# Attention with a gated MLP on one core: new last denominators, x chunk 1 loaded in two parts, other planner numbers for four blocks

## The chip, the cores and the metric

The kernel runs on one core of one Trainium2 chip. The metric is the device time of one execution in microseconds, the median of several. Before the change it is 414.47 us, the median of three runs from 414.26 to 415.19.

## The reference, cut to what matters

```python
x = A_x                                   # 1 x 2048 x 448, bf16
xn = _layernorm(x, axis=-1)
qkv = xn @ wqkv                           # 16 heads of 28
scores = einsum("bhqd,bhkd->bhqk", q, k) * 28 ** -0.5
s = einsum("bhqk,bhkd->bhqd", softmax(scores), v) @ wo
h = gelu(xn @ w1 + b1)                    # 448 -> 1792, tanh form
g = silu(h @ w2 + b2)                     # 1792 -> 448
return x + s * g
```

The softmax's denominator is divided out after the product with v: the kernel sums exp(scores) for each query and head and multiplies the head's output by the reciprocal.

## The kernel before

The 2048 rows are cut into four chunks of 512, the 16 heads (28 wide, padded to 32) into four groups of four. A **block** is one group and one chunk of queries, 16 in all, numbered group by group. A block has 64 **score tiles** (one head of the group by 128 keys by 512 queries), so there are 1024, counted by m. Four heads lie in the four row groups of the PE array, so their score matmuls run side by side (L1700). ACT takes the exponential of two or three tiles in one instruction (L1754); groups of four tiles, the "late" ones, are instead approximated on DVE (L2034 for the scores, L2107 for copies that are added up on PE). Then PE multiplies the exponentials by v (L2282), with a column of twos beside v that yields the denominators. Of all this the layer norm, the projections, the MLP with its gelu (between about 224 and 251 us) and the output projection are spread beside the exponentials.

The order is made when the program is built, by a planner in Python. Each piece of work is a generator that yields tasks with an engine, the buffers that it reads and writes, an estimated duration and a priority; `run` puts down the task that can start first, with rules for priorities, and the instructions go into each engine's queue in that order. The numbers of these rules (`BPN`) are set anew for each block from a row of `BP`; `NQ[b]` is the number of times that the planner tries to make a late group in block b, evenly spaced over its tiles (`p_late`, `pick`). The estimates set the order alone: on the chip every instruction waits on semaphores.

**The start.** `loads` issues x chunk 0 in three parts, the first heads' weights on ACT's and SP's queues (L952), then x chunk 1 whole on SP (L940). `p_ln` takes the statistics of each tile of 128 rows on DVE (`bn_stats`, L1016), `p_ln2` takes the logarithm and the exponential on ACT for the inverse root (L1052, L1054) and normalizes on DVE (L1071); PE transposes (L1204), and ACT or DVE moves the result to xnT (L1216, L1217). The projections follow, and the first scores and exponentials.

ACT's function table is set by name at two places: line 933, before everything (`natural_log_exp_and_others`), and line 1594, after the gelu (`exp_and_others`).

**The tail.** The last block is cut in three parts by queries: 0 to 255, 256 to 383 and 384 to 511. For the third part `p_den` makes the denominators ahead of the product with v: DVE copies what has been accumulated so far (L2194), PE spreads the copy's denominator rows over each head's 32 rows in a bank called `K.den`, and `t_ones` adds the last tiles by matmuls with a matrix of twos (L2227). `p_epi4` copies the sums out of PSUM (L2311 by ACT for this part, L2314 by DVE for the others); `p_norm4` takes the reciprocal on DVE (L2332) and multiplies (L2337). `p_last` projects with wo (through `_mm`, L129), and `t_oev` writes the tile out: either DVE multiplies by the gate from PSUM (L2403), or, for the tiles in `PATH` and after the last exponential has been put down, ACT copies (L2399) and DVE multiplies (L2401); then DVE adds x (L2409) and SP stores (L2413). The gate of the last tile is made beside that: Tanh on ACT (L1661), a product on POOL (L1666), an add on DVE (L1671).

## Time and profile before

| | |
|---|---|
| median of the runs | 414.47 us |
| the profiled execution | 414.64 us |
| its span, first to last instruction | 412.8 us |
| granted TensorE clock | 0.999 |
| first exponential of a score starts | 13.27 us |
| exponentials of scores (L1754) | 354 instructions, 776 tiles of 512 columns |
| approximated on DVE (L2034) | 248 tiles |
| loads of ACT's function table | 3, of 1.28 us each |

Times are microseconds from the first instruction of the profiled execution. PE is the matmul engine, PEld its weight loads, ACT, DVE, POOL and SP the others; a q behind an engine's name is its DMA queue. A group's row shows line, engine, operation, what it writes and reads, shapes, and how many; behind it busy time, the mean in ns and the idle time before, with what ended it. A timeline's row begins with start and length. In the stretches, the columns are the stretch, its length, the busy time of PE, PEld, DVE, ACT and POOL with the number of instructions, the granted clock, the share of the DMA engines and GB/s. An engine's share of the span is an average; what a change is worth is read from the stretch in which it lies.

### The profile page before, as it was taken

The numbers are of one execution on the slowest core, as the hardware profiler recorded it, in microseconds if no ns is written. First come the engines' busy times: TensorE is split into PE (matmuls) and PEld (weight loads), VectorE is DVE, ScalarE is ACT, GpSimd is POOL, SyncE is SP. The second block draws the span as 40 slices with busy tenths as digits, with TensorE's granted clock in tenths as the row PEclk, the third lists the DMA queues.
The fourth block names the chain that finished last, engine by engine and source line by source line (L and its number), as shares of the span: only waits on it lengthen the run. The fifth ranks groups of instructions, "written<-read, shape, count | busy, mean of one in ns | idle before, by whom it ended". The sixth has DMA issues, their size and how long they took to land.

```text
span 412.8 us, 14654 instructions
## 1 busy us (share of the span) xinstructions
PE 394.0 (95%) x6146; PEld 143.4 (35%) x6146; DVE 345.1 (84%) x599; ACT 401.5 (97%) x411; POOL 193.8 (47%) x218
## 2 busy tenths in 40 slices
PE   5999999999999999999999999999999999999995
PEld 3543232333322233232224553332333223333453
DVE  7958798896679888989898117999998999899986
ACT  5899999999999999999999999999999999999995
POOL 6594656649972563255632411156156014553041
PEclk9999999999999999999999999999999999999999
DMA  7801110001000010100330000220010003200073
GB/s 240 301 4 39 6 31 2 23 12 26 21 3 30 2 28 7 33 2 2 100 105 16 28 3 6 54 54 17 16 31 2 29 6 58 72 16 14 18 144 98
DMA packets 18640, 17.56 MB, mean 43 GB/s; under 512 B 8925, under 2 KB 15277, under 8 KB 18542
## 3 DMA queue, kind: packets, MB, share of 16 engines
q1 hardware_dynamic: 16878, 13.78, 11.4%
q0 software_dynamic: 1008, 2.49, 3.5%
q8 instruction: 49, 0.80, 0.8%
q10 hardware_dynamic: 688, 0.34, 0.3%
q14 instruction: 17, 0.14, 0.1%
HBM read 12.54 MB, written 2.88 MB: 37 GB/s over the span
## 4 chain that ended last, share of the span: by engine, by line
PE 71%; ACT 15%; DVE 6%; issue 5%; DMA 1%; POOL 1%; SPq 0%; DVEq 0%; ACTq 0%; POOLq 0%
PE ring L129 33%; PE ring L1700 19%; PE ring L2282 16%; ACT P L1754 8%; ACT h L1754 5%; DMA x_sb<-in_A_x_dram 1%; PE ring L1513 1%; DVE st L1016 1%; ACT xnT L1754 1%; DVE x_sb L2034 1%; PE ring L1122 1%; DVE h L2034 0%; PE ring L1089 0%; POOL h L1075 0%; DVE vaug L1475 0%
## 5 line engine op out<-in xcount | busy, mean ns | idle before, releaser
L1754 ACT ACTIVATE P<-ring 128x1024 bf16<-128x1024 f32 (+1 forms) x235 | 248.9, 1166 | 1.5 <-PE ring L2282 0.3
L1700 PE MATMUL ring<-qT,kT 32*128 32x512 bf16 (+2 forms) x1132 | 131.4, 359 | 5.6 <-ACT P L1754 1.9
L1754 ACT ACTIVATE h<-ring 128x1024 bf16<-128x1024 f32 (+1 forms) x79 | 85.7, 1177 | 0.4 <-PE ring L2282 0.3
L1700 PEld LDWEIGHTS ring<-qT,kT 32*128 32x128 bf16 x1132 | 36.4, 91 | 120.5 <-ACT P L1754 60.4
L2034 DVE TENSOR_SCALAR vaug<-ring 128x512 uint16<-128x512 f32 x88 | 58.6, 685 | 6.6 <-PE ring L1700 4.6
L129 PE MATMUL ring<-xnT,w 128*32 128x512 bf16 x864 | 57.6, 381 | 0.4 <-ACT h L1754 0.2
L129 PE MATMUL ring<-w,h 128*32 128x448 bf16 x896 | 55.5, 355 | 0.2 <-DVE x_sb L2034 0.2
L2282 PE MATMUL ring<-P,vaug 128*32 128x512 bf16 (+2 forms) x599 | 53.7, 352 | 0.1
L2377 POOL TENSOR_TENSOR qT<-x_sb,E_sb 128x512 bf16<-128x512 f32 x15 | 17.8, 1183 | 65.2 <-PE ring L2282 29.0
L2366 POOL TENSOR_TENSOR rc<-rs,mone 128x16 f32<-128x16 bf16 x11 | 32.4, 2947 | 29.2 <-DMA rs<-E_sb 27.6
L1754 ACT ACTIVATE xnT<-ring 128x1024 bf16<-128x1024 f32 (+1 forms) x40 | 44.0, 1128 | 0.0
L2034 DVE TENSOR_SCALAR w<-ring 128x512 uint16<-128x512 f32 x52 | 34.7, 686 | 2.7 <-PE ring L1700 2.1
L129 PEld LDWEIGHTS ring<-xnT,w 128*32 128x32 bf16 x864 | 20.5, 96 | 26.1 <-issue 6.1
L129 PEld LDWEIGHTS ring<-w,h 128*32 128x32 bf16 x896 | 18.0, 95 | 22.8 <-issue 14.0
L2034 DVE TENSOR_SCALAR h<-ring 128x512 uint16<-128x512 f32 x32 | 21.3, 685 | 3.8 <-PE ring L1700 3.6
L2282 PE MATMUL ring<-h,vaug 128*32 128x512 bf16 (+1 forms) x209 | 23.9, 379 | 0.5 <-ACT P L1754 0.4
L1415 DVE CAST qT<-ring 128x512 bf16<-128x512 f32 x15 | 10.3, 689 | 15.3 <-PE ring L129 14.9
L2282 PEld LDWEIGHTS ring<-P,vaug 128*32 128x32 bf16 x599 | 15.9, 95 | 14.3 <-issue 6.9
L1421 POOL TENSOR_TENSOR qsq<-qT 128x512 bf16<-128x512 bf16 x12 | 12.5, 1039 | 17.9 <-DVE qT L1415 17.9
L1527 DVE CAST h<-ring 128x512 bf16<-128x512 f32 x24 | 16.4, 688 | 5.0 <-PE ring L129 4.9
L2034 DVE TENSOR_SCALAR x_sb<-ring 128x512 uint16<-128x512 f32 x28 | 18.6, 683 | 2.5 <-PE ring L1700 1.6
L129 PE MATMUL ring<-xnT,wk 128*32 128x512 bf16 x232 | 17.9, 383 | 0.0
(245 smaller groups left out, 639.6 us busy)
## 6 DMA issues: line engine op xcount, KB each, us to landing
x_sb<-recs SPq DMA_DIRECT2D x60, 64.0 KB, 2.0
w<-in_B_w_dram SPq DMA_DIRECT2D x1, 1568.0 KB, 8.7
x_sb<-in_A_x_dram SPq DMA_DIRECT2D x3, 448.0 KB, 6.8
w<-in_B_w_dram SPq DMA_DIRECT2D x1, 1344.0 KB, 8.1
out_dram<-in_A_x_dram SPq DMA_DIRECT2D x2, 448.0 KB, 10.2
out_dram<-h POOLq DMA_DIRECT2D x4, 224.0 KB, 6.6
out_dram<-h SPq DMA_DIRECT2D x8, 112.0 KB, 1.8
xnT<-wq POOLq DMA_DIRECT2D x1, 512.0 KB, 6.3
```

The lines of the kernel that those rows point to most:

```text
L129: ins = eng.matmul(out[q:q + 32, :], w[:, q:q + 32], x, tile_position=(0, q), start=start, stop=stop, skip_group_check=True)
L1016: yield _Task(DVE, lambda eng, i=i, t=t: eng.bn_stats(K.st6[:, i, :], K.x_sb[:, c, t, :]), [K.b_x[c] if c else K.b_x0[h] if t else K.b_x0t ...
L1122: return eng.matmul(bank, w[sl, 3, g * 128:(g + 1) * 128], K.xnT[sl, 3, c * 512:(c + 1) * 512], tile_position=pos, start=False, stop=True, ...
L1415: yield _Task(DVE, lambda eng: eng.tensor_copy(qb, bank), [tok], [qr], 0.7, 0.0, dp)
L1421: yield _Task(POOL, lambda eng: eng.tensor_tensor(qs, qb, qb, ALU.mult), [qr], [tq], 1.1, 0.05, 2, port=True)
L1527: yield _Task(DVE, lambda eng: eng.tensor_copy(dst, bank), [tok], wr, 0.69, 0.0, 2)
L1700: return eng.matmul(dst, K.kT[32 * j:32 * j + 32, g, t * 128:(t + 1) * 128], K.qT[32 * j:32 * j + 32, g, c * 512 + q0:c * 512 + q0 + nq], ...
L1754: return eng.activation(reg[:, i0:i0 + n, :], src, ACTF.Exp, scale=SM_SCALE)
L2034: yield _Task(DVE, lambda eng: eng.tensor_scalar(K.part(u, k).bitcast(dt.uint16), K.like(u, bank), SM_SCALE * LOG2E * 128.0, (127.0 - EXP_ ...
L2282: return eng.matmul(acc[32 * j:32 * j + 32, q0:q0 + nq], w, ap[:, col:col + nq] if len(ap.shape) == 2 else ap[:, col // 128:(col + nq) // ...
L2366: yield _Task(POOL, lambda eng: eng.tensor_tensor(K.rc[:, :], K.rs[:, :], K.mone[:, 0:1].to_broadcast([128, 16]), ALU.pow), [K.b_srs, K.b_ ...
L2377: yield _Task(POOL, lambda eng: eng.tensor_tensor(dst, K.rb, E, ALU.mult), [K.b_rb, tE], [K.b_onT[g][c]], 1.15, 0.05, 1, port=True)
```

## The change

It has four parts.

- **The start.** x chunk 1 is loaded in two DMAs: its tile 0 on ACT's queue, behind the weights, with a buffer and a semaphore of its own (`b_x1t`, `s_x1t`); tiles 1 to 3 on SP. The statistics and the normalization of that tile wait for the new semaphore.
- **Planner numbers.** Rows 12 to 15 of `BP` get other values (three unused rows at the end go), and `NQ[13]` is 8 instead of 9.
- **The last denominators.** They are made in two PSUM banks, 64 columns each (`RS`), and each of the last matmuls with twos becomes two. DVE takes the reciprocal of the first half; ACT takes the logarithm of the second half and the exponential of its negative. DVE multiplies by the sums straight from PSUM, so ACT's copy of them goes.
- **Output tiles.** (1,3) and (3,2) leave `PATH`, (3,1) joins it; the add of x for (2,0) goes to POOL. A third way of adding x, on PE, is there for tiles in `PADD`, which is empty.

```diff
-    (2, 1, 0, 2.679, 7, 0.134, 1, 0.031, 0.063, 0.302, -0.231, 18, 3, 0.532, 3, 7, 0.134, 4, 7, 4, 7, 0.691, 0.51, 81, 20, 0, 1, 3.888, 2, 0, 7.133, 12, 3.0),
-    (3, 1, 1, 0.982, 7, 0.12, 1.551, 0.011, 0.163, 1.176, 0.806, 12, 3, 0.03, 4, 4, 0.112, 1, 7, 5, 14, 0.77, 0.506, 46, 23, 1, 1, 4.944, 4, 0, 4.0, 33, 2.058),
-    (3, 1, 0, 3.94, 9, 0.129, 1.365, 0.096, 0.166, 0.546, -0.231, 13, 2, 0.532, 1, 7, 0.15, 4, 8, 12, 4, 0.672, 0.667, 75, 16, 1, 1, 4.005, 1, 1, 7.133, 13, 3.12),
-    (2, 1, 1, 2.679, 30, 0.129, 1, 0.096, 0.247, 0.047, 0.61, 13, 5, 0.532, 3, 7, 0.061, 4, 7, 4, 13, 0.821, 0.7, 75, 14, 1, 1, 3.78, 3, 0, 7.133, 24, 3.0),
+    (2, 1, 0, 2.679, 7, 0.134, 1, 0.021, 0.063, 0.302, -0.231, 18, 3, 0.532, 3, 7, 0.134, 4, 7, 4, 7, 0.691, 0.408, 81, 20, 0, 1, 3.888, 2, 0, 7.133, 12, 3.0),
+    (3, 1, 1, 0.982, 7, 0.12, 1, 0.011, 0.163, 1.176, 0.806, 12, 3, 0.03, 4, 4, 0.112, 1, 7, 5, 14, 0.77, 0.506, 46, 23, 1, 1, 4.944, 4, 0, 4.0, 33, 2.058),
+    (3, 1, 0, 3.94, 9, 0.11, 1.365, 0.096, 0.166, 0.546, -0.5, 13, 2, 0.532, 1, 7, 0.099, 4, 8, 12, 4, 0.672, 1.086, 75, 16, 1, 1, 4.005, 1, 1, 7.133, 16, 3.12),
+    (2, 1, 1, 2.679, 30, 0.129, 1, 0.11, 0.247, 0.047, 0.61, 13, 5, 0.532, 3, 12, 0.061, 4, 7, 4, 13, 0.821, 0.7, 75, 14, 1, 1, 4.2, 3, 0, 7.133, 24, 3.0),
-NQ = (14, 4, 4, 4, 7, 14, 7, 16, 8, 15, 5, 9, 6, 9, 12, 8)
+NQ = (14, 4, 4, 4, 7, 14, 7, 16, 8, 15, 5, 9, 6, 8, 12, 8)
+RS = 64
+PADD = ()
-PATH = {(1, 2): 'D', (1, 3): 'D', (2, 0): 'D', (2, 1): 'D', (2, 2): 'D', (2, 3): 'D', (3, 2): 'D', (3, 3): 'D'}
-XADD = ()
+PATH = {(1, 2): 'D', (2, 0): 'D', (2, 1): 'D', (2, 2): 'D', (2, 3): 'D', (3, 1): 'D', (3, 3): 'D'}
+XADD = ((2, 0),)
...
-        ld(K.x_sb[:, 1, :, :], xr[1], K.s_x[1], [K.b_x[1]], 6.5)
+        K.dma(ACT, lambda eng: eng.dma_start(K.x_sb[:, 1, 0, :], xr[1][:, 0, :]), K.s_x1t, writes=[K.b_x1t], land=6.5)
+        ld(K.x_sb[:, 1, 1:4, :], xr[1][:, 1:4, :], K.s_x[1], [K.b_x[1]], 6.5)
...
-        K.den = yield ("bank", lambda: K.ready([K.b_E[0]]), 1)
-        den, td = K.den
-        yield _Task(PE, lambda eng: _mm(eng, den[:, 0:128], K.selb[:, :], Ea, True, False), [K.b_E[0], K.b_selb], [td], 0.1, 0.12, 1)
+        K.den = []
+        for c0, c1 in ((0, RS), (RS, 128)):
+            x = yield ("bank", lambda: K.ready([K.b_E[0]]), 1)
+            K.den.append(x)
+            yield _Task(PE, lambda eng, d=x[0], c0=c0, c1=c1: _mm(eng, d[:, c0:c1], K.selb[:, :], Ea[:, c0:c1], True, False), [K.b_E[0], K.b_selb], [x[1]], 0.08, 0.12, 1)
...
-        if s == 2 and EA:
-            yield _Task(ACT, lambda eng: eng.activation(K.E_sb[:, 1, sl], bank[0][:, sl], ACTF.Copy), [bank[1]],
-                        [K.b_E4[t] for t in ts] + [K.b_E[1]], 0.3, 0.0, 0)
...
+        if s == 2:
+            K.E_done = NBLK - 1 + s
+            yield from K.p_norm3(*bank)
+            K.banks.append(bank)
+            return
...
+    def p_norm3(self, acc, ta):
+        K = self
+        g, c = G - 1, C - 1
+        (d0, td), (d1, te) = K.den
+        R = K.rf[:, 1, :]
+        K.b_rf3.r += K.b_rf[1].r + [K.b_rf[1].w]
+        K.b_rf3.tr = K.b_rf[1].tr
+        yield _Task(ACT, lambda eng: eng.activation(R[:, RS:128], d1[:, RS:128], ACTF.Ln), [te], [K.b_rf3], 0.2 + 0.00085 * (128 - RS), 0.0, 0)
+        yield _Task(DVE, lambda eng: eng.reciprocal(R[:, 0:RS], d0[:, 0:RS]), [td], [K.b_rf[1]], 0.06 + 0.00705 * RS, 0.0, HOT)
+        yield _Task(ACT, lambda eng: eng.activation(R[:, RS:128], R[:, RS:128], ACTF.Exp, scale=-1.0), [], [K.b_rf3], 0.2 + 0.00085 * (128 - RS), 0.0, 0)
+        K.hot = {DVE: max(K.tE[DVE], K.b_rf3.tw + SEM, ta.tw + SEM)}
+        K.banks += K.den
+        dst = K.qT[:, g, c * 512 + 384:c * 512 + 512]
+        yield _Task(DVE, lambda eng: eng.tensor_tensor(dst, acc[:, 384:512], R, ALU.mult), [ta, K.b_rf[1], K.b_rf3, K.b_qT[g][c]],
+                    [K.b_on4[3]], 0.3, 0.0, HOT)
+        K.hot = {PE: K.b_on4[3].tw + SEM}
+        K.hot[DVE] = K.hot[PE] + 0.43
+        K.on4[3] = True
```

More of the change, by code (lines that the diff above doesn't have):

```diff
@@ L422, in run @@
             self.settle()
-            if self.next_m >= MTOT and all(p[3].prio >= 90 if isinstance(p[3], _Task) else p[3][0] == "bank" and self.lq_end and not self.lq for p in self.procs):
+            if self.next_m >= MTOT and not self.px and all(p[3].prio >= 90 if isinstance(p[3], _Task) else p[3][0] == "bank" and self.lq_end and not self.lq for p in self.procs):
                 return
@@ L2218, in t_ones @@
         K = self
-        den, td = K.den
+        cut = (0, RS, 128)
         fl, rd = [], []
@@ L2324, in p_norm4 @@
         E, tE = K.E_sb[:, 1, 128 * t:128 * (t + 1)], K.b_E4[t]
[L2325 to L2330 removed]
+        bank, tok = yield ("bank", lambda: K.g_done[C - 1] and K.ready([tE]), 3)
+        yield _Task(PE, lambda eng: _mm(eng, bank[:, 0:128], K.selb[:, :], E, True, True),
+                    [tE, K.b_selb], [tok], 0.1, 0.12, 3)
         R = K.rf[:, t % 2, :]
[L2332 to L2334 removed]
+        yield _Task(DVE, lambda eng: eng.reciprocal(R, bank[:, 0:128]), [tok], [K.b_rf[t % 2]], 0.96, 0.0, 1)
         K.banks.append((bank, tok))
@@ L2406, in t_oev, with f @@
         ov = K.out[0].rearrange("(c p t) d -> c p t d", p=128, t=4)[c]
-        if own:
+        if own and (c, t) in PADD and way:
+            K.px += 1
+            bank, tk = yield ("bank", lambda: K.ready([wr]), 1)
+            xx = K.x2[0][t] if c == C - 2 else K.x2[1][:, t, :]
+            def f(eng):
+                _mm(eng, bank[:, 0:D], K.ident[:, :], xx, True, False)
+                return _mm(eng, bank[:, 0:D], K.ident[:, :], o, False, True)
+            yield _Task(PE, f, [K.b_x2[c], K.b_id, wr], [tk], 0.38, 0.17, 1)
+            yield _Task(ACT, lambda eng: eng.activation(o, bank[:, 0:D], ACTF.Copy), [tk], [wr], 0.48, 0.0, 1)
+            K.banks.append((bank, tk))
+            K.px -= 1
+            K.outs.append(K.dma(SP, lambda eng: eng.dma_start(ov[:, t, :], o), K.s_out[6 + t if c == C - 1 else t + 10], reads=[wr]))
+            K.fin = max(K.fin, wr.tw + 2.2)
+        elif own:
             E = POOL if (c, t) in XADD else DVE
```

45 lines of the change are left out of this document (18 added, 27 removed), and 2 rows, old and new, of the table BP.

## The prediction, on record before the change was run

> **What bounds the kernel now.** I read the page's busy shares first, then the busy time by stretch, then the timeline of each engine at the two ends of the kernel, since the change edits both ends by hand and the middle only through numbers of the planner.
>
> ```profile
> PE 394.0 (95%) x6146; PEld 143.4 (35%) x6146; DVE 345.1 (84%) x599; ACT 401.5 (97%) x411; POOL 193.8 (47%) x218
> PE 71%; ACT 15%; DVE 6%; issue 5%; DMA 1%; POOL 1%; SPq 0%; DVEq 0%; ACTq 0%; POOLq 0%
> 290.00:330.00 40.00, 39.36 (x572) 12.62 (x570) 38.17 (x64) 39.89 (x43) 13.84 (x11) 1.00 0.06 16
> 330.00:355.00 25.00, 24.83 (x363) 8.15 (x361) 24.52 (x38) 24.89 (x24) 8.79 (x8) 1.00 0.18 40
> 355.00:380.00 25.00, 24.40 (x366) 8.27 (x364) 22.07 (x37) 25.00 (x23) 12.54 (x12) 1.00 0.10 31
> 380.00:395.00 15.00, 15.00 (x328) 7.39 (x329) 13.52 (x24) 14.76 (x16) 0.40 (x1) 1.00 0.19 53
> 395.00:407.00 12.00, 11.91 (x366) 6.74 (x362) 9.37 (x20) 11.67 (x14) 4.36 (x6) 1.00 0.65 121
> 407.00:412.80 5.80, 1.54 (x30) 0.56 (x18) 3.32 (x9) 1.86 (x4) 0.92 (x1) 0.96 0.23 75
> 284.94 3.77 ACT L1754 ACTIVATE P<-ring 128x1024 bf16<-128x1024 f32 x4 [0.28 <-PE ring L2282]
> 288.57 1.98 ACT L1754 ACTIVATE xnT<-ring 128x1024 bf16<-128x1024 f32 x2
> ```
>
> ACT is the fullest engine: 401.5 of 412.8 us. The chain of waits puts most of its share on PE, but in the five stretches from 290 to 407 us ACT is without work for only 0.11, 0.11, 0.00, 0.24 and 0.33 us, together 0.79 us. PE and DVE wait for it there and it for them in turn; what moves the end is ACT's amount of work, its first exponential and what follows its last one. The last two rows give the price of that work: four exponentials of two score tiles each start at 284.94 and the next at 288.57, so 3.63 / 8 = 0.45 us a tile. A group of four tiles that the planner gives to DVE instead (a "late" group) is worth 1.8 us of ACT. The last stretch is another regime: 5.8 us with every engine mostly idle, a plain serial tail.
>
> The profiled execution took 414.64 us with a span of 412.8 us; the median of the three runs is 414.47. I add the terms to the former and take off 0.17 at the end.
>
> **Part 1, the start.** The load of x chunk 1 is cut: its first tile goes out on ACT's queue with a semaphore of its own, three tiles stay on SP.
>
> ```profile
> 1.19 0.98 ACTq L952 DMA_DIRECT2D h<-in_A_wqkv_dram  x2
> h<-in_A_wqkv_dram ACTq DMA_DIRECT2D x2, 56.0 KB, 3.0
> 6.50 0.15 DVE L1028 TENSOR_SCALAR mv<-st 128x1 f32<-128x1 f32 x1
> 7.01 0.20 ACT L1054 ACTIVATE rstd<-lnv 128x2 f32<-128x2 f32 x1
> 7.52 0.63 DVE L1016 BATCH_NORM_STATS2 st<-x_sb 128x6 f32<-128x448 bf16 x1 [0.87 <-DMA x_sb<-in_A_x_dram]
> 7.88 0.56 ACT L1148 ACTIVATE wk<-h 128x448 bf16<-128x448 bf16 x1
> 8.07 0.69 DVE L1071 TENSOR_SCALAR h<-x_sb,mv,rstd 128x448 bf16<-128x448 bf16 x2
> 8.87 0.24 PEld L1204 LDWEIGHTS ring<-ident,h 128*128 128x128 bf16 x4 [1.38 <-DVE h L1071]
> 9.32 0.60 ACT L1216 ACTIVATE xnT<-ring 128x512 bf16<-128x512 bf16 x1 [0.88 <-PE ring L1204]
> 13.27 1.00 ACT L1754 ACTIVATE P<-ring 128x1024 bf16<-128x1024 f32 x1
> 0.00:13.30 13.30, 8.57 (x130) 6.05 (x131) 10.78 (x45) 8.08 (x23) 9.81 (x30) 1.00 0.86 260
> ```
>
> DVE is done at 6.65, then stands 0.87 us for that chunk, because the statistics of its first tile (L1016) are ahead of the normalization of chunk 0 (L1071) in DVE's queue. L1071 has had its factor since 7.21, so the stall delays the transposes (8.87, idle for L1071) and the second half of xnT (9.32, idle for the transposes). The new load is issued behind the two on ACT's queue, at 2.17, and those took 3.0 us to land: about 5.2 to 5.7 for a load of 112 KB, before 6.65. Then the statistics run 6.65 to 7.28, L1071 starts at about 7.3 rather than 8.07, the transposes 0.8 us earlier; ACT is free for them at 8.44 (its copy of wk ends), when they end. What is late next is DVE's own work, which moves along. Bounds: 0.8 us gained; nothing, or 0.4 us lost, if the earlier 112 KB only push the others back (112 KB at the 260 GB/s of this stretch). I take **0.7 us gained**, near the measured stall, as ACT is full from 13.27 on.
>
> **Part 2, the middle.** Four rows of planner numbers for blocks 12 to 15 change, and block 13 may try for 8 late groups instead of 9. No row shows what order comes out. One late group more or less is worth 1.8 us as worked out above; beyond that a better order can win the 0.79 us of ACT's idle time and little else. The pace in block 13 falls from one try in 52/9 = 5.8 tiles to 6.5, and DVE, at 24.52 of 25 us from 330 to 355, limits these groups there more than the number of tries does. `PADD` is empty, so the branch it opens adds nothing. I take **0, with -1.8 and +1.8 as ends**.
>
> **Part 3, the tail.** The rows from the last exponential on:
>
> ```profile
> 406.22 0.59 ACT L1661 ACTIVATE w<-w 128x448 bf16<-128x448 bf16 x1
> 406.40 0.24 PE L2227 MATMUL ring<-xnT,one 128*32 128x128 bf16 x2
> 406.87 0.96 DVE L2332 RECIPROCAL w<-ring 128x128 f32<-128x128 f32 x1 [0.89 <-PE ring L2227]
> 407.07 0.28 ACT L2311 ACTIVATE E_sb<-ring 128x128 bf16<-128x128 f32 x1 [0.26 <-PE ring L2282]
> 407.45 0.54 ACT L2399 ACTIVATE h<-ring 128x448 bf16<-128x448 f32 x1
> 407.93 0.29 DVE L2337 TENSOR_TENSOR qT<-E_sb,w 128x128 bf16<-128x128 bf16 x1
> 408.20 1.04 ACT L2399 ACTIVATE h<-ring 128x448 bf16<-128x448 f32 x2 [0.21 <-PE ring L129]
> 408.27 0.10 PEld L129 LDWEIGHTS ring<-wo,qT 128*32 128x32 bf16 x4 [0.55 <-DVE qT L2337]
> 409.77 0.69 DVE L2409 TENSOR_TENSOR h<-h 128x448 bf16<-128x448 bf16 x2
> L1234 ACT ACTIVATE kT<-ring 128x256 bf16<-128x256 f32 x2 | 0.8, 384 | 0.2 <-PE ring L1225 0.2
> ```
>
> The serial chain is: sums on PE, reciprocal (0.96), product at 407.93, projection at 408.27, copy, gate, add, store, end at 412.8, which is 4.87 us after the product starts. The change puts three things in place of the 0.96 us. DVE's half, 64 columns, is half of the row: 0.5 us, ready at 407.4. ACT's half is Ln and Exp of 64 columns: from 277 ns for 128 columns (0.28) and 384 ns for 256 the price is 0.84 ns a column, so 0.22 us each. If that were all, the product would start at 406.87 + 0.22 + 0.22 + 0.10 (the gap from reciprocal to product now) or at 407.4 + 0.10: 407.5, a gain of 0.4 us.
>
> But the logarithm needs a function table, and these rows show its price:
>
> ```profile
> 219.96 4.36 ACT L1754 ACTIVATE P<-ring 128x1024 bf16<-128x1024 f32 x4
> 224.34 1.28 ACT L1589 ACT_TABLE_LOAD   x1
> 225.63 1.48 ACT L1589 ACTIVATE h<-h 128x1536 bf16<-128x1536 bf16 x1
> 251.47 1.28 ACT L1594 ACT_TABLE_LOAD   x1
> 252.77 1.02 ACT L1754 ACTIVATE P<-ring 128x1024 bf16<-128x1024 f32 x1
> ```
>
> The code names a set at line 933 (for Ln and Exp together) and at line 1594 (exp_and_others, which stays to the end). The load at L1589 stands in no line of the code: it was put in ahead of the gelu because the set did not have it, and it began as soon as the engine was free. So Ln after line 1594 gets a load too. Whether the set that is put in for Ln also has Exp no row shows; nothing in the new code names the joint set, as line 933 had to, so I take it that each function gets a set by itself: **two loads**. Then: Tanh ends at 406.81, load to 408.11, Ln to 408.34, load to 409.64, Exp to 409.87, product at 409.97 instead of 407.93: **2.0 us lost**. ACT's copies of output tiles (L2399, at 407.45 and 408.20) stand behind Exp on its queue, but the last tile's copy is due at about 410.75, by which time two of 0.54 us have gone through; DVE, whose adds (two in 0.69 us) came last, is idle until then, so at most 0.2 us come back. With one load the product starts at 408.34 + 0.22 + 0.10 = 408.7: 0.75 us lost.
>
> The Trainium skill, page "ScalarE: Activation LUTs", section "What ACT_TABLE_LOAD costs", counts 1283 ns for the load and 1380 ns of drain, about 2.66 us a switch. This trace agrees with the first and not with the whole: from the load at 251.47 to the next exponential at 252.77 are 1.30 us. By the page two switches would cost 5.3 us and the tail about 2.7 us more than I sum.
>
> At nothing I cost: the E copy that ACT no longer makes (0.28 us at 407.07, beside the reciprocal); the sums cut in two banks, twice the matmuls at half the columns (at most 0.2 us, under the loads that now come last; if these are absent, 0 to 0.2 us lost); the product read from PSUM; tile (2,0)'s add on POOL (its 0.69/2 us on DVE would become about 1 us, covered by the 4.9 us after the product). Which tiles go through ACT ((1,3), (3,2) no longer, (3,1) new) touches only those that come after the last exponential, three now; without cover each is one 0.54 us copy.
>
> **The sum:** -0.7 + 0 + 2.0 = +1.3; 414.64 + 1.3 - 0.17 = **415.8 us**.
>
> **The rivals.**
> - One load serves both (not slower). For it: the joint set exists, line 933 uses it for both functions with no load between L1052 and L1054. Against: here nobody names it. -0.7 + 0.75 = 0: 414.5.
> The Trainium skill gives this result: "ScalarE activation tables: per-element evaluation and per-set limits", section "Table sets in the compiler and the runtime", says that loads are placed by the longest run that one set serves. The trace has no unnamed pair that could show it.
> - No load is exposed, or a late group is gained (faster, the other side). The mechanism: one group of four tiles moves from ACT to DVE in blocks 14 or 15, where DVE has 2.93 us free in 355 to 380; it decides from the point at which 1.8 us exceed the tail's loss less the start's gain. With two loads 414.0, with one 412.7. With no load at all -0.7 - 0.4: 413.4. Against: DVE is full one block earlier, and the tries in block 13 are fewer.
> - A late group is lost: 417.6. For it: fewer tries, DVE at 24.52 of 25 us.
> - The start does not pay: the 112 KB delay the weights, 416.5 to 416.9. For it: the DMA share is 0.86 in that stretch.
> - A switch costs 2.66 us with drain: 418.5. Against: the two switches above.
>
> **How the numbers follow.** Forecast (two loads, order of blocks 12 to 15 within half a group) 0.45; one load 0.20; late group gained 0.12 (0.07 of it with two loads); group lost 0.10; no load 0.04; start not paying 0.06; long switch 0.03. Bounds for "same" are 0.2%, 0.83 us, about what a measurement of this kernel can tell from no change: 413.64 to 415.30. Faster: no load 0.04, group gained with one load 0.05, half of the gained groups with two loads 0.04, a fifth of the one-load case 0.04: 0.17. Same: the rest of the one-load case, less a fifth on its slow side, 0.12, the other gained groups 0.03, and a quarter of the forecast 0.11, where the order wins some of ACT's 0.79 us: 0.26. Slower: the rest, 0.57. Leaving out 1 in 10 at each end gives 413.2 to 417.7.
>
> **What would show it.** Right: two ACT_TABLE_LOAD rows by Ln and Exp near the end, the product (TENSOR_TENSOR of 128x128) starting 2.0 us later after the last exponential than now (1.71 us after 406.22), DVE's half reciprocal of about 0.5 us; the statistics' wait of 0.87 us gone and the first exponential near 12.5; the count of tiles in DVE's L2034 groups about the same. Wrong: one load or none in the tail; a first exponential still near 13.3; or ACT's exponentials more or fewer by a group, which alone outweighs the start.

## The result and the profile after

The changed kernel takes 416.30 us (median of six runs, 415.73 to 417.68), the kernel before 414.37 us on the same chip (six runs, 414.13 to 415.19): a ratio of 1.0047 with a 95% interval of 1.003 to 1.0063. It is slower, by 0.5%, clear of the interval. Executions of one kernel differ by about 2 us, and part of that goes with the granted clock: of twelve runs of start_only (below) the three with a mean clock of 0.993 to 0.996 took 415.57 to 415.84 us, the other nine 413.99 to 414.72. The profiled execution took 416.29 us with a span of 414.5 us, 1.7 us more than before's.

The page's shares of busy time and of the chain of waits, which answer to the first two rows shown of before:

```profile
PE 394.3 (95%) x6169; PEld 143.4 (35%) x6169; DVE 346.2 (84%) x598; ACT 403.8 (97%) x413; POOL 195.8 (47%) x219
...
PE 58%; ACT 24%; issue 8%; DVE 8%; POOL 1%; DMA 1%; DVEq 0%; ACTq 0%; POOLq 0%
```

ACT has two instructions and 2.3 us more (401.5 before), and its share of the chain has grown from 15% to 24%. Where this lies the timelines show. First the tail, on the timeline of ACT in the kernel after (start, length, engine, line, operation, how many, then the idle time before and what ended it):

```profile
404.10 2.36 ACT L1756 ACTIVATE P<-ring 128x1024 bf16<-128x1024 f32 x2
406.33 0.59 ACT L1663 ACTIVATE w<-w 128x448 bf16<-128x448 bf16 x1
406.94 1.28 ACT L2351 ACT_TABLE_LOAD   x1
408.23 0.22 ACT L2351 ACTIVATE w<-ring 128x64 f32<-128x64 f32 x1
408.47 1.28 ACT L2353 ACT_TABLE_LOAD   x1
409.77 0.26 ACT L2353 ACTIVATE w<-w 128x64 f32<-128x64 f32 x1
409.93 0.53 ACT L2418 ACTIVATE h<-ring 128x448 bf16<-128x448 f32 x1
410.93 0.54 ACT L2418 ACTIVATE h<-ring 128x448 bf16<-128x448 f32 x1 [0.47 <-PE ring L128]
```

and the timeline of DVE there:

```profile
407.60 0.56 DVE L2352 RECIPROCAL w<-ring 128x64 f32<-128x64 f32 x1 [0.55 <-PE ring L2234]
410.15 0.29 DVE L2357 TENSOR_TENSOR qT<-ring,w 128x128 bf16<-128x128 f32 x1 [2.00 <-ACT w L2353]
```

DVE's half of the reciprocals is ready at 408.16 (407.60 + 0.56). The product waits 2.00 us, and the releaser in brackets is ACT's exponential: behind the Tanh of 406.33 stand two loads of the function table, one for Ln and one for Exp. Between Tanh and product lie 3.82 us; before, 1.71. Behind the last exponential there are now two copies by ACT (L2418) where there were three, and from the product to the end of the span are 4.34 us instead of 4.89: behind the product DVE has two multiplications by the gate and two additions of x where it had three and three.

Then the start and the middle. The first fence is DVE's timeline of the kernel after, at the statistics that waited 0.87 us before. The second is ACT's there: the first exponential, the place at which most of the start's gain was lost, and the exponentials near 403 us.

```profile
6.55 0.62 DVE L1018 BATCH_NORM_STATS2 st<-x_sb 128x6 f32<-128x448 bf16 x1
7.30 0.98 DVE L1073 TENSOR_SCALAR h<-x_sb,mv,rstd 128x448 bf16<-128x448 bf16 x2
```

```profile
12.80 1.92 ACT L1756 ACTIVATE P<-ring 128x1024 bf16<-128x1024 f32 x2
...
50.18 1.02 ACT L1756 ACTIVATE h<-ring 128x1024 bf16<-128x1024 f32 x1 [0.30 <-PE ring L1702]
...
397.14 5.66 ACT L1756 ACTIVATE P<-ring 128x1024 bf16<-128x1024 f32 x6
403.18 1.02 ACT L1756 ACTIVATE xnT<-ring 128x1024 bf16<-128x1024 f32 x1 [0.38 <-PE ring L1702]
```

The wait is gone and the first exponential starts 0.47 us earlier than before (13.27). By "lead" I mean how much earlier than in the kernel before the same exponential starts. It stays at 0.46 us up to 49 us, is 0.10 us behind the idle time at 50.18 and stays there up to about 377 us. By the count of tiles it grows to 0.5 us at 390 to 394 us, where the new rows act, and by the last exponential it is -0.11: Tanh starts at 406.33 instead of 406.22. The stretches of the kernel after (busy us of PE, PEld, DVE, ACT, POOL) show ACT full as before up to 395, and idle for 0.64 us instead of 0.33 behind that:

```profile
380.00:395.00 15.00, 14.50 (x316) 6.45 (x310) 13.78 (x25) 15.00 (x17) 1.07 (x1) 1.00 0.18 53
395.00:407.00 12.00, 11.48 (x356) 6.65 (x357) 9.63 (x20) 11.36 (x14) 4.65 (x6) 1.00 0.68 126
```

So the 1.67 us of span (414.49 - 412.82) are 0.11 up to Tanh, plus 2.11 from Tanh to product, less 0.55 behind the product. The number of DVE's approximated tiles (248) did not change.

### The profile page after: what moved, and what is told of

Its sections match the earlier page's. It is cut to its first block, busy times and chain, and to the rows that moved or that the text cites. A ratio compares the mean times of both kernels' runs of the same rounds, so it can differ in the third digit from the quotient of the medians.

```text
span 414.5 us, 14713 instructions
## 1 busy us (share of the span) xinstructions
PE 394.3 (95%) x6169; PEld 143.4 (35%) x6169; DVE 346.2 (84%) x598; ACT 403.8 (97%) x413; POOL 195.8 (47%) x219
## 4 chain that ended last, share of the span: by engine, by line
PE 58%; ACT 24%; issue 8%; DVE 8%; POOL 1%; DMA 1%; DVEq 0%; ACTq 0%; POOLq 0%
PE ring L128 28%; PE ring L1702 15%; ACT P L1756 13%; PE ring L2289 13%; ACT h L1756 7%; ACT xnT L1756 2%; DVE st L1018 1%; PE ring L1515 1%; DVE x_sb L2036 1%; DMA x_sb<-in_A_x_dram 1%; DVE w L2036 0%; DVE h L2036 0%; PE ring L1091 0%; DVE h L2109 0%; DVE w L2337 0%
## 5 line engine op out<-in xcount | busy, mean ns | idle before, releaser
L1702 PEld LDWEIGHTS ring<-qT,kT 32*128 32x128 bf16 x1131 | 35.5, 91 | 120.2 <-ACT P L1756 60.2
L2036 DVE TENSOR_SCALAR vaug<-ring 128x512 uint16<-128x512 f32 x92 | 61.1, 683 | 5.9 <-PE ring L1702 3.8
L1756 ACT ACTIVATE xnT<-ring 128x1024 bf16<-128x1024 f32 (+1 forms) x39 | 43.0, 1130 | 0.6 <-PE ring L1702 0.6
L2289 PE MATMUL ring<-h,vaug 128*32 128x512 bf16 x201 | 23.4, 383 | 0.5 <-ACT P L1756 0.4
L2036 DVE TENSOR_SCALAR h<-ring 128x512 uint16<-128x512 f32 x28 | 18.7, 685 | 3.8 <-PE ring L1702 3.6
L128 PE MATMUL ring<-wo,qT 128*32 128x448 bf16 x256 | 16.0, 355 | 2.4 <-DVE qT L2357 2.3
```

The source lines that it names most:

```text
L128: ins = eng.matmul(out[q:q + 32, :], w[:, q:q + 32], x, tile_position=(0, q), start=start, stop=stop, skip_group_check=True)
L1702: return eng.matmul(dst, K.kT[32 * j:32 * j + 32, g, t * 128:(t + 1) * 128], K.qT[32 * j:32 * j + 32, g, c * 512 + q0:c * 512 + q0 + nq], ...
L1756: return eng.activation(reg[:, i0:i0 + n, :], src, ACTF.Exp, scale=SM_SCALE)
L2036: yield _Task(DVE, lambda eng: eng.tensor_scalar(K.part(u, k).bitcast(dt.uint16), K.like(u, bank), SM_SCALE * LOG2E * 128.0, (127.0 - EXP_ ...
L2289: return eng.matmul(acc[32 * j:32 * j + 32, q0:q0 + nq], w, ap[:, col:col + nq] if len(ap.shape) == 2 else ap[:, col // 128:(col + nq) // ...
```

## The experiments

Twelve kernels, each timed beside the kernel before on the same chip. The kernel before had medians of 414.88 us beside the first four of them in the table, 414.75 beside the next four and 415.04 beside the last four, so kernels are compared by the ratios, not by the medians. The theory: the two loads are the loss, the start is a small gain, the rows do nothing. The main rival: the sums come late, and set the tail; further rivals say where the start's gain went. The table has the medians with the ratio to before, and from each profile the start of the first exponential, the start of Tanh, the time from Tanh to the last product, and from there to the end (all us).

| kernel | median | ratio (95%) | first exp. | Tanh | to product | to end |
|---|---|---|---|---|---|---|
| before | | | 13.27 | 406.22 | 1.71 | 4.89 |
| after | 416.30 | 1.0047 (1.003–1.0063) | 12.80 | 406.33 | 3.82 | 4.34 |
| start_only | 414.50 | 0.9987 (0.9975–0.9999) | 12.60 | 405.55 | 1.71 | 4.89 |
| numbers_only | 414.49 | 0.9989 (0.9976–1.0002) | 12.98 | 406.35 | 2.05 | 4.34 |
| tail_only | 417.67 | 1.0057 (1.0037–1.0077) | 12.80 | 405.73 | 3.82 | 5.45 |
| joint_set | 414.89 | 1.0002 (0.9989–1.0014) | 12.74 | 406.39 | 2.54 | 4.34 |
| old_tail | 414.58 | 0.9985 (0.9968–1.0002) | 12.62 | 406.20 | 2.05 | 4.33 |
| dve_halves | 414.91 | 1.0000 (0.9983–1.0016) | 12.77 | 406.32 | 2.38 | 4.34 |
| b1_first | 416.32 | 1.0033 (1.0017–1.0049) | 12.68 | 406.32 | 3.83 | 4.53 |
| start_b1 | 415.03 | 0.9998 (0.9983–1.0014) | 13.04 | 406.70 | 1.71 | 4.89 |
| start_path | 415.16 | 1.0006 (0.9991–1.002) | 12.73 | 406.04 | 2.10 | 4.33 |
| path_only | 415.88 | 1.0019 (1.0002–1.0037) | 13.39 | 406.85 | 2.00 | 4.34 |
| bp_only | 415.14 | 1.0005 (0.9987–1.0022) | 13.02 | 407.18 | 2.18 | 5.37 |
| psum_product | 414.50 | 0.9988 (0.9972–1.0004) | 12.64 | 406.00 | 2.06 | 4.32 |

The runs of one kernel spread over more than most of these differences (start_only: 413.99 to 415.84), so a ratio within 0.0015 of 1 says little by itself, and a profile is one execution.

**start_only: the cut load alone, in the kernel before.**

```diff
-        ld(K.x_sb[:, 1, :, :], xr[1], K.s_x[1], [K.b_x[1]], 6.5)
+        K.dma(ACT, lambda eng: eng.dma_start(K.x_sb[:, 1, 0, :], xr[1][:, 0, :]), K.s_x1t, writes=[K.b_x1t], land=6.5)
+        ld(K.x_sb[:, 1, 1:4, :], xr[1][:, 1:4, :], K.s_x[1], [K.b_x[1]], 6.5)
```

> The kernel before with only the cut load of x chunk 1. Both theories: the first exponential starts near 12.8 us instead of 13.27, as in the changed kernel. Theory A (the start's gain is taken back at 49 us, where the cast of b1 on POOL waits for a DMA that lands no earlier and then runs into DVE): the lead of ACT falls from 0.47 to about 0.1 us between 45 and 52 us, the time is 0.1 us under the kernel before, within noise. Theory B (the loss at 49 us belongs to the other edits of the changed kernel): the lead stays 0.47 to the last exponential, and the time is 0.5 us under the kernel before, 413.9.

The wait is gone, and the whole lead of 0.67 us at the first exponential (13.27 to 12.60) is still there at Tanh (406.22 to 405.55). The median is 0.13% below before's. So with before's order a lead lasts to the end, in this execution: theory B, in the profile. At 49 us the bias comes late here too (POOL's cast starts at 44.90, after 2.45 us of waiting), but not late enough to cost ACT anything.

**numbers_only: the rows, `NQ` and the choice of output tiles, in the kernel before.**

```diff
-NQ = (14, 4, 4, 4, 7, 14, 7, 16, 8, 15, 5, 9, 6, 9, 12, 8)
+NQ = (14, 4, 4, 4, 7, 14, 7, 16, 8, 15, 5, 9, 6, 8, 12, 8)
...
+PATH = {(1, 2): 'D', (2, 0): 'D', (2, 1): 'D', (2, 2): 'D', (2, 3): 'D', (3, 1): 'D', (3, 3): 'D'}
+XADD = ((2, 0),)
```

> The kernel before with only the planner's numbers and the choice of output tiles (rows of BP, NQ, PATH, XADD). Theory A (the new order of the last two blocks is no better: in the changed kernel ACT waits 0.24 and 0.38 us for scores between 395 and 404 us): the last exponential starts 0.1 to 0.4 us later than before, the time is 414.4 to 414.9. Theory B (the numbers help, and the tail alone loses): the last exponential starts 0.3 us or more earlier, the time is 414.1 or less.

No measurable difference in time, but not because nothing changes. Without the new denominators and the cut load, the new order already loses on ACT near 403 us, has the sums 0.34 us later behind Tanh, and gets 0.55 us back behind the product. The rows of ACT and DVE in numbers_only:

```profile
396.96 5.65 ACT L1752 ACTIVATE P<-ring 128x1024 bf16<-128x1024 f32 x6
403.19 1.02 ACT L1752 ACTIVATE xnT<-ring 128x1024 bf16<-128x1024 f32 x1 [0.58 <-PE ring L1698]
...
406.35 0.59 ACT L1659 ACTIVATE w<-w 128x448 bf16<-128x448 bf16 x1
```

```profile
407.34 0.96 DVE L2330 RECIPROCAL w<-ring 128x128 f32<-128x128 f32 x1 [0.27 <-PE ring L2225]
```

Here the reciprocal starts 0.99 us behind Tanh, in the kernel before 0.65.

**tail_only: the new last denominators alone, in the kernel before** (`p_den`, `t_ones`, `p_epi4` and `p_norm3` as in the change; before's rows, tiles and load).

```diff
+        for c0, c1 in ((0, RS), (RS, 128)):
+            x = yield ("bank", lambda: K.ready([K.b_E[0]]), 1)
...
+            yield from K.p_norm3(*bank)
```

> The kernel before with only the new last denominators (two banks, half of the reciprocal by Ln and Exp, product from PSUM). Theory A (two table loads put the product with the reciprocal 2.0 us later): two ACT_TABLE_LOAD rows after the Tanh, the product 3.5 to 3.9 us after the Tanh's start instead of 1.71, the time 1.6 to 2.0 us over the kernel before, 416.0 to 416.4. Theory B (the tail is slow because PE makes the sums late: DVE's reciprocal starts 1.27 us after the Tanh's start in the changed kernel, 0.65 before): the same loads, but the product moves with the sums, and a tail whose sums come as early as before loses under 1 us.

The rows of tail_only on ACT, and on DVE:

```profile
405.73 0.59 ACT L1664 ACTIVATE w<-w 128x448 bf16<-128x448 bf16 x1
406.33 1.28 ACT L2352 ACT_TABLE_LOAD   x1
407.87 1.28 ACT L2354 ACT_TABLE_LOAD   x1
```

```profile
406.51 0.56 DVE L2353 RECIPROCAL w<-ring 128x64 f32<-128x64 f32 x1 [1.02 <-PE ring L2235]
409.55 0.29 DVE L2358 TENSOR_TENSOR qT<-ring,w 128x128 bf16<-128x128 f32 x1 [2.48 <-ACT w L2354]
```

The sums come 0.78 us behind Tanh here and 1.27 in the kernel after, and the product is 3.82 us behind Tanh in both. So the loads set the product and the rival of the late sums does not, as long as the loads are there. Its ratio, 1.0057, lies above the whole change's 1.0047, with intervals that overlap. The median, 417.67 us, is more than the 416.0 to 416.4 of theory A (the profiled run took 416.82): the end behind the product, which theory A took as it was, is the longest of all, 5.45 us. PE's last row in tail_only:

```profile
409.90 1.10 PE L130 MATMUL ring<-wo,qT 128*32 128x448 bf16 x12 [2.45 <-DVE qT L2358]
```

Twelve matmuls of the projection stand behind the product here, four in the kernel before and in the kernel after. They take 1.10 us, where 12 of them took 0.74 at 398.79 in the kernel after; the granted clock is 0.71 between 410.0 and 410.4 and 0.50 up to 411.0. ACT's last two copies wait for them.

**joint_set: the kernel after, with the set that has both functions named ahead of Ln.**

```diff
+        K.prog[ACT].append(lambda eng: eng.preload_act_table_set("natural_log_exp_and_others"))
         yield _Task(ACT, lambda eng: eng.activation(R[:, RS:128], d1[:, RS:128], ACTF.Ln), ...)
```

> The changed kernel with the set that holds both logarithm and exponential named ahead of Ln, so one load instead of two. Theory A (the loads set the time of the product): one ACT_TABLE_LOAD row in the tail, Exp ends 1.3 us earlier, the product starts near 408.8 instead of 410.15, the time falls by 1.3 us against the changed kernel, to 415.0. Theory B (late sums set it): DVE's half reciprocal starts where it does now, 1.27 us after the Tanh, and the time falls by 0.3 us at most.

ACT's rows in joint_set:

```profile
407.00 1.28 ACT L2351 ACT_TABLE_LOAD   x1
408.29 0.22 ACT L2352 ACTIVATE w<-ring 128x64 f32<-128x64 f32 x1
408.55 0.26 ACT L2354 ACTIVATE w<-w 128x64 f32<-128x64 f32 x1
```

One load, and the product 2.54 us behind Tanh instead of 3.82: 1.28 us less, exactly one load. The time falls to before's (1.0002). This is the clearest run of the study: one named set, nothing else, takes away the loss that the times show. In the profile 0.45 us of span are left over before's (413.27 against 412.82).

**old_tail: the kernel after with before's denominators,** so start, rows and tiles without the new tail (its `p_den`, `t_ones`, `p_epi4`, `p_norm4` are before's).

```diff
-            yield from K.p_norm3(*bank)
...
+        yield _Task(DVE, lambda eng: eng.reciprocal(R, bank[:, 0:128]), [tok], [K.b_rf[t % 2]], 0.96, 0.0, HOT if t == 3 else 1)
```

> The changed kernel with the tail of the kernel before: cut load, planner's numbers and output tiles stay, the last denominators are made in one bank with one reciprocal on DVE and ACT's copy of the sums. Theory A (the loss is the tail's alone, the rest is even): 414.2 to 414.6, no table load after the gelu's. Theory B (the numbers lose too): 414.8 or more.

The ratio is 0.9985 (0.9968 to 1.0002), the product 2.05 us behind Tanh as in numbers_only. The new tail therefore costs 3.82 - 2.05 = 1.77 us against the old one in the same order, and one load of it (joint_set) 2.54 - 2.05 = 0.49.

**dve_halves: the kernel after, with both halves of the reciprocal on DVE,** so two banks and the product from PSUM, but no function of ACT.

```diff
-        yield _Task(ACT, lambda eng: eng.activation(R[:, RS:128], d1[:, RS:128], ACTF.Ln), ...)
-        yield _Task(ACT, lambda eng: eng.activation(R[:, RS:128], R[:, RS:128], ACTF.Exp, scale=-1.0), ...)
+        yield _Task(DVE, lambda eng: eng.reciprocal(R[:, RS:128], d1[:, RS:128]), ...)
```

> The changed kernel with both halves of the reciprocal on DVE, one after the other (two banks and the product from PSUM stay; no logarithm, no exponential). Theory A (the two loads are the cost, and the sums come 0.6 us late beside them): no table load in the tail, the product near 407.6 + 0.56 + 0.50 + 0.1 = 408.75 instead of 410.15, the time 1.4 us under the changed kernel, about 414.9. Theory B (without the loads the tail is as designed, better than the kernel before): 414.0 or less.

DVE's rows in dve_halves:

```profile
407.60 0.56 DVE L2351 RECIPROCAL w<-ring 128x64 f32<-128x64 f32 x1 [0.55 <-PE ring L2234]
408.07 0.49 DVE L2352 RECIPROCAL w<-ring 128x64 f32<-128x64 f32 x1
408.70 0.29 DVE L2356 TENSOR_TENSOR qT<-ring,w 128x128 bf16<-128x128 f32 x1
```

Theory A's 408.75 and 414.9 came out (408.70, 414.91). With no load the product is 2.38 us behind Tanh, 0.33 later than with one reciprocal in one bank (old_tail). The reciprocals start 1.28 us behind Tanh against 0.99. What the two banks cost on PE stands in its timeline, first in the kernel after and then in old_tail:

```profile
405.58 1.31 PE L128 MATMUL ring<-wo,qT 128*32 128x448 bf16 x24
406.71 0.23 PE L128 MATMUL ring<-E_sb,selb 128*32 128x64 bf16 x8
406.77 0.71 PE L2234 MATMUL ring<-P,one 128*32 128x64 bf16 x29
```

```profile
405.45 1.31 PE L127 MATMUL ring<-wo,qT 128*32 128x448 bf16 x24
406.59 0.23 PE L127 MATMUL ring<-E_sb,selb 128*32 128x128 bf16 x4
406.64 0.43 PE L2226 MATMUL ring<-P,one 128*32 128x128 bf16 x16
```

Twice as many matmuls of half the columns are not half as long each: from the first of the sums' matmuls to the reciprocal are 0.89 us with two banks and 0.60 with one (406.59 to 407.19). And in both, 24 matmuls of the output projection (1.31 us) stand ahead of the sums on PE. So the rival of the late sums is true of something: without loads it is what is left, and the half reciprocal beside Ln and Exp could have won at most 2.05 - (1.28 + 0.56 + 0.10) = 0.1 us, with 0.10 the gap from reciprocal to product as before. No run has that tail.

**b1_first: the kernel after, with the load of the bias b1 issued ahead of the 16 pieces of wo.** The lead of the kernel after is lost at 49 us, where POOL waits for that bias. The rows of POOL and of DVE in the kernel after:

```profile
45.78 0.20 POOL L871 CAST b1c<-b1h 128x14 f32<-128x14 bf16 x1 [3.10 <-DMA b1h<-in_B_b_dram]
45.95 2.04 POOL L2103 TENSOR_TENSOR h<-w,shc 128x512 int32<-128x512 int32 x2
```

```profile
47.12 1.41 DVE L2109 TENSOR_SCALAR h<-w 128x2048 uint16<-128x2048 uint16 x1
```

The bias lands late, POOL's two adds start late, and DVE's operation, 0.69 us long elsewhere, takes 1.41 us beside them. PE and then ACT (0.30 us idle at 50.18) wait for it. This is a matter of the single execution: in the twelve profiles in which b1 is loaded behind wo, POOL's cast starts anywhere between 43.39 and 45.78 us, and ACT loses time there in two of them, the kernel after (45.78) and old_tail (45.66).

```diff
+            yield ("until", lambda: K.b_b1h.tw is not None)
             K.wait(SP, K.b_wo.w)
```

> The changed kernel with the 16 loads of wo issued on SP after the two loads of b1 instead of ahead of them. Theory A (the start's gain is lost at 49 us because b1 lands no earlier than before): POOL's wait of 3.1 us for b1 is gone, the DVE instruction that took 1.41 us there takes 0.69, the lead of 0.47 us holds to 377 us, and the time is 0.35 us under the changed kernel. Theory B (the collision comes from the order of work, not from b1): the same loss near 49 us and no change of time.

The rows of POOL and of DVE in b1_first:

```profile
42.50 0.42 POOL L871 CAST b1c<-b1h 128x14 f32<-128x14 bf16 x1
43.37 2.04 POOL L2104 TENSOR_TENSOR h<-w,shc 128x512 int32<-128x512 int32 x2 [0.45 <-DVE qsq L1426]
```

```profile
47.00 0.69 DVE L2110 TENSOR_SCALAR h<-w 128x2048 uint16<-128x2048 uint16 x1
```

The wait is gone, the operation takes 0.69 us and the lead of 0.59 us now lasts up to 377 us. So theory A is right about the loss at 49 us, and wrong about the time: the ratio is 1.0033 against 1.0047, with intervals that overlap, and Tanh starts at 406.32, as in the kernel after (406.33). The lead only goes later: ACT waits 0.87 us near 403, in b1_first as follows.

```profile
396.66 5.64 ACT L1757 ACTIVATE P<-ring 128x1024 bf16<-128x1024 f32 x6
403.16 1.02 ACT L1757 ACTIVATE xnT<-ring 128x1024 bf16<-128x1024 f32 x1 [0.87 <-PE ring L1703]
```

```profile
402.24 0.28 PE L1703 MATMUL ring<-qT,kT 32*128 32x128 bf16 x3
...
402.81 0.32 PE L1703 MATMUL ring<-qT,kT 32*128 32x128 bf16 x5 [0.28 <-issue]
```

The six exponentials ahead of it start at 397.14 in the kernel after, at 396.96 in numbers_only and at 396.66 here; the one behind them at 403.18, 403.19 and 403.16. So near 403 these three executions meet something that does not come earlier when ACT does; it is not fixed in time either, for in psum_product, with the same order there, the exponential comes at 402.85. PE's second row has idle time that the profile puts down to "issue", to no engine's work. What holds PE there was not settled. One rival that no run tests: the DMA engines are as good as full there (share 1.07 and 0.94 in the half microseconds from 402.0 and from 402.5), and the profile's DMA queues include one for instructions, so PE's own may have come late.

The end behind the product is 4.53 us here instead of 4.34 because the last four matmuls of the projection take 0.56 us instead of 0.37; between 410.4 and 410.6 the granted clock is 0.53, in the kernel after 1.00.

**start_b1: the cut load and the earlier bias in the kernel before** (the edits of start_only and b1_first).

```diff
+            yield ("until", lambda: K.b_b1h.tw is not None)
...
+        K.dma(ACT, lambda eng: eng.dma_start(K.x_sb[:, 1, 0, :], xr[1][:, 0, :]), K.s_x1t, writes=[K.b_x1t], land=6.5)
```

> The kernel before with the cut load of x chunk 1 and the loads of b1 issued ahead of wo's. Theory A: the first exponential near 12.8, the lead of 0.47 us kept to the last exponential, the time 413.9 (0.47 us under the kernel before). Theory B: the lead is lost elsewhere and the time is that of the kernel before.

The ratio is 0.9998 (0.9983 to 1.0014). Here the lead of 0.23 us is lost as well, in before's order. PE's row in start_b1:

```profile
403.14 0.46 PE L2284 MATMUL ring<-P,vaug 128*32 128x128 bf16 x20 [0.55 <-issue]
```

and Tanh is at 406.70, 0.48 us behind before's. So a hold near 403 us can come with before's rows and tiles too; and the earlier bias, which cured the loss at 49 us, is worth nothing that the times show.

**start_path, path_only and bp_only: numbers_only and the start taken apart.** path_only has the choice of output tiles and POOL's add in the kernel before; start_path the cut load as well; bp_only the rows and `NQ` without the tiles. The edit of the tiles is first below, for path_only and start_path; that of bp_only second.

```diff
+PATH = {(1, 2): 'D', (2, 0): 'D', (2, 1): 'D', (2, 2): 'D', (2, 3): 'D', (3, 1): 'D', (3, 3): 'D'}
+XADD = ((2, 0),)
```

```diff
+NQ = (14, 4, 4, 4, 7, 14, 7, 16, 8, 15, 5, 9, 6, 8, 12, 8)
```

> The kernel before with the cut load of x chunk 1 and the new choice of output tiles (PATH, XADD) alone; planner's rows, NQ and the last denominators as before. Theory A (the new choice of tiles is what shortens the stretch from the product to the end from 4.89 to 4.34 us, and the planner's rows are what loses 0.3 us and more before it): first exponential near 12.75, the last one 0.5 us ahead of the kernel before, the product 1.7 us after the Tanh, 4.34 us to the end: 413.5, the fastest of all. Theory B (rows and tiles only work together): the stretch to the end stays 4.9 us or the product comes later, 414.2 or more.

> The kernel before with the new choice of output tiles alone. Theory A: 4.34 us from the product to the end, the rest as before, 413.9. Theory B: no better than the kernel before, 414.4 or more.

> The kernel before with the planner's rows 12 to 15 and NQ alone. Theory A: ACT's waits for scores between 395 and 404 us are there as in the run with rows and tiles, the last exponential is 0.4 us later against the first one than in the kernel before, 414.8. Theory B: the waits come with the tiles and not with the rows, and the time is 414.4 or less.

The tiles alone make the end behind the product shorter by 0.55 us (4.89 to 4.34 in path_only, 4.33 in start_path), but bring the sums later (2.00 and 2.10 us from Tanh to product), so 0.29 to 0.39 us of it are given back at once. And they lose time ahead of Tanh. ACT's row in start_path:

```profile
403.74 1.02 ACT L1755 ACTIVATE P<-ring 128x1024 bf16<-128x1024 f32 x1 [0.52 <-PE ring L1701]
```

Between 377 us and Tanh the lead falls by 0.37 us in start_path and by 0.52 in path_only; in start_only and tail_only, which have before's rows and tiles, it does not fall at all. So both theories A (413.5 and 413.9) failed, and path_only is the slowest without a load (1.0019).

The rows alone, in bp_only, have four copies by ACT behind the last exponential and 5.37 us to the end, and the ratio is 1.0005. Its late Tanh (407.18) is not the rows' doing. One stretch of bp_only:

```profile
218.00:220.00 2.00, 2.00 (x24) 0.46 (x20) 0.26 (x1) 1.38 (x3) 2.00 (x2) 0.50 0.00 0
```

The granted clock is 0.50 there, with PE busy throughout, and ACT waits for scores: its lead goes from 0.25 us at 215 to -1.11 at 224 us, long before blocks 12 to 15. This run took 416.54 us, where the median is 415.14. From 377 us to Tanh the rows alone gain 0.15 us.

Taken together, the profiles sort ACT's waits behind 394 us. One of 0.24 or 0.25 us near 396 us (397 in bp_only) stands in all eight profiles with the new rows and in no other. The one near 403 us (404 in path_only), 0.38 to 0.87 us, stands in all nine with the new tiles; bp_only has none there, and of those with before's rows and tiles only start_b1 has one over 0.14 us. So the waits near 403 come with the tiles, as theory B for bp_only has it, though its time of 414.4 or less did not come; why the tiles do it was not settled. Together, in numbers_only, rows and tiles make 0.9989, by the ratios better than either alone; but the intervals of these kernels overlap or touch, so the profiles carry this more than the times.

path_only also shows how much the old load's wait varies. DVE's row in path_only, the same instruction as before's 0.87 us:

```profile
7.64 0.63 DVE L1016 BATCH_NORM_STATS2 st<-x_sb 128x6 f32<-128x448 bf16 x1 [1.00 <-DMA x_sb<-in_A_x_dram]
```

In the five profiles with the old load the wait is 0.87, 0.12, 0.49, 1.00 and 0.35 us (before, numbers_only, tail_only, path_only, bp_only) and the first exponential at 13.27, 12.98, 12.80, 13.39 and 13.02: mean 13.09. In the nine with the cut load there is no wait, and the mean is 12.74 (12.60 to 13.04). The cut load gains about 0.35 us at the first exponential.

**psum_product: old_tail with the product straight from PSUM,** without ACT's copy of the sums.

```diff
+        if s == 2:
+            yield from K.p_norm4(3, bank)
...
-        yield _Task(DVE, lambda eng: eng.tensor_tensor(dst, E, R, ALU.mult), [tE, ...])
+        yield _Task(DVE, lambda eng: eng.tensor_tensor(dst, acc[0][:, 384:512], R, ALU.mult), [acc[1], ...])
```

> The run with the old tail (cut load, planner's rows, output tiles), but the last product reads the sums from PSUM and ACT's copy of them goes; it leaves one bank and one reciprocal. Theory A (the copy was beside the reciprocal, so reading PSUM moves nothing): the product 2.05 us after the Tanh as with the copy, 414.5. Theory B (the product from PSUM costs or saves by itself): the product's length differs from 0.29 us by over 0.1, or the time from that of the old tail by over 0.3 us.

DVE's row in psum_product:

```profile
408.06 0.29 DVE L2338 TENSOR_TENSOR qT<-ring,w 128x128 bf16<-128x128 f32 x1
```

The product takes 0.29 us from PSUM, as it did from the copy, and comes 2.06 us behind Tanh (old_tail 2.05): the copy lay beside the reciprocal and cost nothing. The ratio is 0.9988 (0.9972 to 1.0004).

No kernel of the study is faster than the one before by more than an interval's edge. start_only is the only one whose interval ends below 1 (0.9999).

## Why the prediction was right, and where it was wrong

The time came out half a microsecond above the forecast, by a sum of which one term was right and two were wrong in opposite directions. That the total came so near is in part luck.

**The tail to the product: right, step by step.** Two loads, of 1.28 us each, behind Tanh; Ln 0.22 as forecast, Exp 0.26 instead of 0.22, half a reciprocal 0.56 instead of 0.5. The product moved by 2.11 us behind Tanh where +2.04 was forecast. That each function gets a set by itself was a choice with no row behind it; joint_set shows that it was the choice that mattered, and that the one-load rival's product was priced well too (2.48 us behind Tanh forecast, 2.54 measured). The rival's rule, of the Trainium skill, page "ScalarE activation tables: per-element evaluation and per-set limits", section "Table sets in the compiler and the runtime", would have given one load for Ln and Exp side by side; the trace of after has two. The Trainium skill's page "ScalarE: Activation LUTs", section "What ACT_TABLE_LOAD costs", would have made each switch 2.66 us; here it is 1.30 us, from the load at 408.47 to Exp at 409.77.

**"At most 0.2 us come back": wrong, 0.55 us did.** The failed step is "at nothing I cost ... which tiles go through ACT", together with the copies' count: I took it that three copies stay behind the last exponential. With the new tiles there are two (path_only, which has the tiles alone, as well), and the end behind the product is 4.32 to 4.34 us in every kernel with the new tiles, with the new rows or without, save b1_first's 4.53, and 4.89 to 5.45 in those with the old ones. The reason given, that copies behind Exp still end in time, was wrong too. By the prediction's own numbers two of 0.54 us behind an Exp that ends at 409.87 end at 410.95, later than the 410.75 at which the last is due. tail_only, which has the loads with before's tiles, shows that nothing comes back there: its end is 0.56 us longer than before's, though there it is PE's projection that holds the copies up. So beside the two loads the new tiles are worth 5.45 - 4.34 = 1.11 us, a part of it because of the lower clock in tail_only.

**"The sums cut in two banks ... at most 0.2 us": right in kind, small.** It is 0.29 us (0.89 against 0.60), hidden under the loads. That the new rows and tiles bring the sums later by another 0.34 us (0.65 to 0.99 from Tanh to the reciprocal) I did not see at all; it was hidden in the same way.

**The no-load rival (product 1.28 us behind Tanh): wrong, if it were to be had.** It left the sums where they were. Worked out from dve_halves' rows the product would come 1.94 us behind Tanh at best, 0.1 better than with one reciprocal; no run shows it.

**Part 1, the start: right mechanism, wrong size, and wrong that it must reach the end.** The wait went; the first exponential came 0.47 us earlier instead of 0.7, and 0.35 over all profiles. The term was sized from one execution whose wait (0.87) was the second longest of five. The step "as ACT is full from 13.27 on" failed besides: ACT is full, but at single places it waits for PE, and a lead can be lost there. In the kernel after 0.36 us of it went at 49 us to a late bias, and in b1_first and start_b1 it went near 403 us; in start_only it lasted.

**Part 2, the middle: right that no late group comes or goes, wrong at 0.** 248 tiles on DVE, in both. But the start's gain of 0.47 was a loss of 0.11 by the last exponential, 0.58 us that no term held, within the ends given: 0.36 went at 49 us, and behind 394 us more than the new rows had won up to there. That second loss goes with the new rows near 396 us and with the new tiles near 403.

The sum by what was measured: +0.11 + 2.11 - 0.55 = +1.67, against +1.3. The term that was too good by 0.8 us (start and middle) and the one that was too bad by 0.55 us (what comes back) nearly cancel. What the runs leave open: why the new tiles make ACT wait near 403 us and what holds PE there, and so whether the start's gain could be kept together with the new rows. ACT's Ln and Exp with no load exposed (the joint set brought in earlier, or Tanh replaced) was not tried.

## What to carry to other kernels

Before giving ACT another function, list the sets that its instructions use in the order of its queue, and name the set that holds both if two of them follow each other: here one line was worth 1.28 us of a tail. A half that is moved to another engine only helps by the time at which its input is there, so look first at what stands ahead of that input. And size a wait that ends with a DMA from several executions: here the same wait was 0.1 to 1.0 us.

## What the runs showed of the hardware

- A load of the table begins 0.02 us after ACT's last instruction ended, whether or not the instruction that needs it could start: in the kernel after it began at 406.94, before the sums were there (407.60). It takes 1.28 us and the next instruction starts 0.01 to 0.02 us behind it. So a load can lie beside a wait: one of the two did, for about 0.66 us, and that is why the late sums did not show.
- DVE's copy of 128x2048 (0.69 us) took 1.41 us in the kernel after, and 1.48 in old_tail, where it ran beside POOL's integer adds (45.95 to 47.99 in the kernel after). No run takes the adds away, but the bias, landing earlier or later, moved them. In the five profiles in which the operation took longer, 0.73 to 1.48 us, it began before POOL's second add had ended, and each time it ended 0.54 or 0.55 us behind that add, as in start_only below (47.65 and 47.10); in the other nine it took 0.68 or 0.69 us. The Trainium skill, page "SBUF — State Buffer", section "SBUF: two separate sides", says that GpSimd's operations and some of DVE's lock a shared pair of ports against each other for a whole instruction. The trace agrees as far as this goes; that this operation is one of those no run shows.

```profile
45.07 2.03 POOL L2102 TENSOR_TENSOR h<-w,shc 128x512 int32<-128x512 int32 x2
46.91 0.74 DVE L2108 TENSOR_SCALAR h<-w 128x2048 uint16<-128x2048 uint16 x1
```

- The granted clock can fall in the midst of work: in bp_only it was 0.50 from 218 to 220 us with PE busy throughout, and ACT came out 1.36 us later. Behind PE's wait of 2.45 us in tail_only's tail it fell to 0.50 as well.
- Half the columns are not half the time for short matmuls: 16 sums' matmuls of 128 columns in 0.43 us, 29 of 64 columns in 0.71.
